# Two of a last group's norms by VectorE, and first products in parts by groups of lines

## The chip, the cores and the metric

One core of a Trainium2 chip runs one program. The metric is the device time of one execution in microseconds (us). The engines named below are PE (TensorE, with PEld for its weight loads), DVE (VectorE), ACT (ScalarE), POOL (GpSimd) and SP (SyncE, which issues most DMAs here). Every engine works through its own instructions in the order in which they were written into its queue and waits on semaphores for the others.

## The reference

Four layers work on an array of 2048 lines of 512 numbers: A, B, A, B. Each one normalizes every line, transforms, and adds the result to the array.

```python
def _A_ref(x, w_r, w_i):
    X = rfft2(x, axes=(-2, -1))
    X = X * (w_r + 1j * w_i)
    return irfft2(X, s=(S, D), axes=(-2, -1))

def _B_ref(u, ...):
    K = einsum("dn,dnl,dn->dl", Cc, exp(logdA[:, :, None] * l), dB).real
    y = irfft2(rfft2(pad(u^T)) * rfft2(pad(K)))[..., :L]     # a long convolution per channel
    return y^T + u * Dskip

x = x + _A_ref(_layernorm(x), A_w_r, A_w_i)
x = x + _B_ref(_layernorm(x), ...)
x = x + _A_ref(_layernorm(x), A_w_r, A_w_i)
x = x + _B_ref(_layernorm(x), ...)
```

The layer norm has no weights: (x - mean) / sqrt(var + 1e-5) over the 512 numbers of a line.

## The kernel before

The array lies on the chip as `x`, 128 partitions by 16 by 512. Here a "line" is one of the 16 indices `s2`, and stands for 128 rows at once. Lines 4i to 4i+3 form group i, four groups in all.

The program has four stages, each with its own list in `ORDER`. The first makes the convolution kernel of layer B (`unit_k`, `rows_k` and others, 32 units) and beside it the first layer A (`forward_a`, `first_a`, `inv_a`), and ends with the norms in front of layer B. The second is the first pass of layer B (r = 0), the third the second layer A, with the norms in front of the last layer, the fourth the second pass of layer B (r = 1).

A stage is a set of pieces, each a generator that emits a few instructions between two `yield`s; what it yields says which engine and buffers it needs next and which events must lie behind it. The class `Clock` writes the order: it keeps a model of the time of each engine, and of all pieces that could go on within a short time from the earliest (the first number of a list in `ORDER`) it takes the one with the lowest rank. A rank is the piece's own number in the first list of its entry, plus a shift from the second list for each later step. The ranks are thus not times; they decide between pieces that are ready together. The order is made when the program is written; on the chip the queues are fixed.

What happens in front of a pass of layer B: `inv_a` adds a line of layer A to `x` (L911 to L913) and takes its statistics on VectorE (`moments`, L591 and L592). When the four lines of a group have theirs, `spread` takes the root on ScalarE (L625), and on VectorE the reciprocal `rs` (L627) and `nb` = -mean * rs (L629). Then `norm_b` writes each line normalized into `xn`, on ScalarE as scale and bias from `rs` and `nb` (L639, in `norm`; L641 is the same norm on VectorE, from the mean and `rs`, which no caller uses before).

`forward_b` multiplies a block of 32 channels of all 16 lines by a table of 128 columns: two matmuls, one for each half of the partitions, each 64 rows by 512 columns (L951). There are 16 such products a pass, and VectorE transposes each result out of PSUM into `P` (L955); the first eight go into the left half. `step_b` works on a half when its eight blocks are there: a product with a table (`spectrum`, L963), in the first pass also one for the convolution kernel's rows (L979 loads them, through a ring of three buffers), the multiplication with the kernel's spectrum (L996, L999, L1003), the product back (L1011), and ScalarE's copy into `P` (L1018). `turn_b` (L1034) and `inv_b` (L1050, L1055) bring the result back to lines; `close_b` takes statistics or writes the output (L1064).

At the end of the first stage a unit ends on GpSimd (L1269, L1270), a product (L1282) and a copy (L1291); `rows_k` multiplies the rows (L1309), transposes them on VectorE (L1313) and stores them (L1316). Then SP loads the tables of layer B (L934, L935).

Of the kernel before, what the change touches and what calls it, by code (L numbers as in the profile page):

```python
# [37 lines left out]
LAND, RATE = 2.0, (320e3, 210e3, 250e3)  # L38

ORDER = [  # L40
    (0.050611, {"load_in": ([-48.73, -49.67, -13.2, 200.39, 38.48], [21.36, 0]),
             "load_n": ([170.88], [17.74, 32.32, 39.11, 0]),
             "load_ra": ([122.74], [-34.24, -26.17, 0]),
             "load_h": ([189.13], [-1.1, 0]),
             "load_da": ([87.12], [11.37, 0]),
             "load_rb": ([156.61], [-6.7, 0]),
             "polar_k": ([188.86], [0, 0, -10.23, 4.9, 30.71, 8.86, -8.44, 0]),
             "octant_k": ([195.76], [0, 0, 30.82, 0]),
             "log_k": ([198.17], [7.12, -1.53, 0]),
             "phase_k": ([54.98], [9.47, -22.65, -34.9, -26.84, -10.4, 0]),  # L50
             "parts": ([-1.02, 52.39, 180.27], [-16.65, -3.98, -14.47, -25.06, -3.65, 0]),
             "load_k": ([0.46, 24.35, 26.66, 90.14, 113.68, 14.97, 134.95, 135.35], [-10.85, -5.26, 0]),
             "exp_k": ([31.12, 30.01, 26.72, -30.41, 4.2, 26.79, 11.64, 78.24, -6.3, 0.57, 130.4, 110.04, 7.61, 12.56, -2.93, 102.4, -2.77, 13.49, 75.18, 23.12, 30.66, 48.47, 2.53, 144.61, -3.85, 206.61, 15.72, 29.43, 103.43, 4.73, 22.38, 4.74, 79.71, 78.57, 136.47, 110.99, 104.63, 0.06, 9.23, -3.76, 152.2, 80.58, 107.2, 21.85, 20.82, 98.84, 202.47, 24.5], [-0.87, -2.09, 0]),
             "unit_k": ([-5.49, 9.8, -46.86, 52.48, -7.95, 46.43, 63.91, 65.15, -59.42, -20.7, 96.11, -25.05, -14.14, 82.98, 95.72, 99.58, 47.51, 48.51, 62.41, 78.63, 79.81, 82.78, 85.31, 89.29, 89.73, 95.21, -3.54, 105.55, 118.51, 120.91, 137.32, 137.55], [34.37, 31.83, 13.78, 42.41, 30.07, 30.15, 32.23, 39.12, 35.89, 0]),
             "rows_k": ([48.24, 146.28, 190.46, 133.31, 5.29, 9.15, 119.72, 143.74], [-28.96, -21.87, -21.87, -15.39, -19.71, -19.24, 0]),
             "sums": ([68.3, 174.15, 8.23, 16.19], [32.48, 30.78, 32.04, 16.99, 13.91, 7.66, 34.05, -0.27, 37.66, 2.46, 0]),
             "spread": ([17.55, 129.21, 18.82, 50.21, 18.68, 37.9, 26.12, 42.83, 81.35], [-14.02, -12.43, 0]),
             "moments": ([48.6, 168.25, 167.06, 170.68], [-35.07, 0]),
             "forward_a": ([237.18, 160.57, 32, 190.87, 212.59, 50.71, -0.81, 157.11, 67.95, -12.81, 211.5, 73.12, 9.09, 134.47, 112.18, 101.62], [-41.16, -32.05, -34.91, -48.86, -16.07, 0]),
             "first_a": ([-4.49, -18.8, 15.57, 3.63, 80.21, 17.42, 26.99, 60.31, 117.89, 120.37, 101.06, 141.83, 161.84, 119.48, 213.35, 138.85], [-2.64, 38.82, -12.59, 0.61, 1.12, 22.42, 1.12, 9.82, -0.59, 0.31, 31.16, 0]),  # L60
             "inv_a": ([119.1, 153.39, 154.78, -12.8, 176.52, 180.93, 165.04, 176.64, 179.21, 212.81, 173.77, 172.16, 165.73, 204.44, 203.24, 205.17], [6.59, 5.52, -33.78, -0.86, 39.16, 4.18, 0]),
             "norm_b": ([134.64, -13.39, 180.42, -19.04, 155.44, 123.24, 118.52, -19.66, -9.73, 62, -15.3, 11.32, -33.63, 181.42, 143.72, 95.73], [3.13, 0]),
             "tables": ([52.58], [-16.4, 0])}),
# [7 lines left out]
    (0.010000, {"load_du": ([164.21], [-44.93, 0]),
             "first_a": ([179.48], [-24.75, -4.44, -14.35, 0, 72.12, 2.11, 1.29, 6.33, 6.76, 0.12, 14.34, 0]),
             "group_a": ([194.01, 232.24, 217.79, 202.63, 238.5, 131.16, 205.2, 199.29, 233.37, 217.41, 208.36, 198.07, 122.44, 202.74, 207.67], [-103.75, -39.32, -54.25, -22.22, -23.2, -100.35, -23.93, -3.71, -36.68, -38.02, -25.08, -23.93, 0]),
             "inv_a": ([180.35, 141.51, 145.93, 197.94, 183.36, 101.66, 176.36, 118.03, 147.61, 232.02, 160.93, 213.63, 186.51, 139.07, 199.6, 146.8], [55.08, 1.48, -4.95, -5.13, 25.36, -6.18, -13.95, 0]),
             "spread": ([177.02, 157.89, 140.63, 190.66], [0, -2.36, 0]),
             "norm_b": ([139.04, 206.02, 221.71, 116.37, 218.26, 121.3, 209.11, 190.78, 125.49, 189.55, 217.69, 200.09, 212.22, 217.5, 116.15, 186.47], [-0.59, 0])}),
    (0.191249, {"forward_b": ([16.74, -30.74, 7.86, -14.65, -23.43, -19.05, -24.28, -7.05, 54.87, 33.03, -16.53, 38.87, 21.87, -22.87, 3.42, -24.9], [-14.33, 68.5, 0]),
             "step_b": ([-48.3, -52.59, -66.06, -59.51, -63.91, -44.14, -38.35, -44.74, -47.06, -34.23, -22.73, -28.22, -1.93, -46.76, 16.96, 16.68], [16.57, 35.26, 26.88, 18.48, 44.4, 11.44, 27.32, 94.94, 0]),
             "turn_b": ([-14.27, -34.14, 44.25, 43.22, 23.59, 43.79, -0.43, 14.42, -40.01, 29.56, 38.77, 2.4], [13.89, 0]),
             "inv_b": ([20.94, 61.81, 32.87, 19.49, -33.55, 25.49, 9.2, -18.63, 60.91, -35.33, 1.86, -32.68, 12.23, 21.87, 69.24, 30.39], [76.77, -10.14, 0]),  # L80
             "close_b": ([-46.35, -28.26, 12.32, -60.23, -24.23, 4.46, -64.62, -57.64], [30.99, 0])}),
# [403 lines left out]
class Net:  # L485
# [451 lines left out]

    def norm_b(self, r, s2, st):

        yield "ACT", self.after((id(st), s2)), self.emitted(("group", 1), 16) if r else self.emitted("product", 32)  # L940
        self.norm(s2, st, True, self.xn[r][:, s2, :])
        self.mark("norm_b", r)

    def forward_b(self, r, i):
# [4 lines left out]
        for h in range(2):
            o = slice(64 * h, 64 * h + 64)  # L950
            nc.tensor.matmul(p[:, 512 * h:512 * h + 512], self.Rb[o, :], self.xn[r][o, :, 32 * i:32 * i + 32], start=True, stop=True)  # L951
# [3 lines left out]
        nc.vector.transpose(self.P[r][e][:, :, o:o + 32].rearrange("p k d -> p d k"), p.rearrange("p (s d) -> p d s", s=32))  # L955
# [557 lines left out]
```

## Time and profile before

| | |
|---|---|
| median of 3 runs | 712.26 us (711.82 to 712.85) |
| profiled execution: its time | 709.7 us |
| profiled execution: its span | 707.9 us |
| mean granted clock of TensorE | 0.927 |
| busy: PE, DVE, ACT, POOL | 580.8, 546.8, 425.8, 314.9 us |
| instructions | 19921 |
| read from and written to HBM | 62.51 and 27.13 MB |
| first product of the first pass of layer B | 344.47 us |
| first product of the second pass of layer B | 598.54 us |

The span goes from the first to the last instruction of the core; the execution's time is 1.8 us longer. A row of the timeline gives start, length, engine, line, operation, output and input by the program's names with their shape, the count, and in brackets how long the engine stood idle before it and for whom. A row of a list of groups gives the busy time of the group, the mean length of one instruction in nanoseconds, and the idle time before it. The granted clock is the share of its full rate that TensorE was given.

### The profile page before, as it was taken

Reading aid. Unit: us, or ns where it says so; the run is one execution under the profiler, and the core shown is the slowest. Engines: PE = TensorE matmul, PEld = TensorE weight load, DVE = VectorE, ACT = ScalarE, POOL = GpSimd, SP = SyncE. Lnnn points to the kernel's source line nnn. Section 1 sums busy time; section 2 is a strip of 40 time slices with the busy share of each in tenths; the row PEclk is TensorE's granted clock in tenths of the full one; section 3 lists DMA queues with packets and bytes.
Section 4 is the critical chain, followed back from the end, with each engine's and each line's share of the span. In section 5 each row is a group of like instructions: output and inputs, shape, how many; then the busy total and the mean of one; then the engine's idle time right before and its main releaser. Section 6 shows DMA issues by size and latency. Waiting matters only on the chain. (4 is left out here: it accounts for less than half of the span.)

```text
span 707.9 us, 19921 instructions
## 1 busy us (share of the span) xinstructions
PE 580.8 (82%) x8424; PEld 372.5 (53%) x8424; DVE 546.8 (77%) x807; ACT 425.8 (60%) x742; POOL 314.9 (44%) x299
## 2 busy tenths in 40 slices
PE   0768988989979999796689998579999981789965
PEld 0767866557544444344236564178778750246621
DVE  1697738787697999988694698876988596984994
ACT  6898369898878969787426553067564436035510
POOL 0652108477294462646024562076665670057710
PEclk9969989999999999887699999779999995999996
DMA  8707443221106520101575876260564013025376
GB/s 211 213 16 239 155 130 96 83 74 53 61 25 193 172 75 2 60 4 62 200 274 186 267 243 191 62 262 1 188 228 146 1 44 134 1 92 170 120 213 189
DMA packets 45857, 90.92 MB, mean 128 GB/s; under 512 B 3944, under 2 KB 25960, under 8 KB 44744
## 3 DMA queue, kind: packets, MB, share of 16 engines
q1 hardware_dynamic: 35016, 77.07, 34.4%
q10 hardware_dynamic: 10752, 12.58, 5.0%
q8 instruction: 66, 1.08, 0.6%
q14 instruction: 23, 0.19, 0.1%
HBM read 62.51 MB, written 27.13 MB: 127 GB/s over the span
## 5 line engine op out<-in xcount | busy, mean ns | idle before, releaser
L1003 POOL TENSOR_TENSOR wk<-wk 128x1024 f32<-128x1024 f32 x32 | 75.9, 2380 | 122.7 <-ACT wk L999 122.7
L1269 POOL TENSOR_TENSOR Y<-wk,Y 128x1024 f32<-128x1024 f32 x32 | 76.7, 2396 | 56.2 <-issue 27.6
L1011 PE MATMUL ps<-wk 32*64 32x256 f32 x2048 | 69.7, 381 | 2.5 <-DVE wk L996 0.9
L951 PE MATMUL ps<-Y,cRb 64*128 64x512 f32 x128 | 37.4, 698 | 29.3 <-ACT Y L639 21.7
L1011 PEld LDWEIGHTS ps<-wk 32*64 32x64 f32 x2048 | 47.1, 131 | 26.0 <-issue 7.7
L996 DVE TENSOR_TENSOR wk<-ps,wk 128x1024 f32<-128x1024 f32 x32 | 38.9, 1220 | 24.9 <-PE ps L963 20.3
L1247 DVE SCALAR_TENSOR_TENSOR wk<-wk,ps 128x1024 f32<-128x1024 f32 x32 | 38.9, 1214 | 22.7 <-ACT wk L1245 22.5
L1282 PE MATMUL ps<-Y 128*32 128x64 f32 x2048 | 39.4, 234 | 14.6 <-POOL Y L1270 11.8
L1231 ACT ACTIVATE Y<-ps 128x1024 f32<-128x1024 f32 x48 | 47.7, 1033 | 4.8 <-PE ps L1215 4.5
L1282 PEld LDWEIGHTS ps<-Y 128*32 128x32 f32 x2048 | 34.2, 119 | 29.9 <-POOL Y L1270 21.1
L1215 PE MATMUL ps<-wk,Y 96*128 96x512 bf16 x128 | 40.6, 394 | 8.4 <-ACT Y L1231 4.8
L1050 PE MATMUL ps<-Y,cRbT 128*64 128x512 f32 x128 | 34.5, 692 | 13.9 <-DMA Y<-yi 7.2
L1270 POOL TENSOR_TENSOR Y<-wk,Y 128x512 f32<-128x512 f32 x32 | 43.6, 1363 | 0.0
L999 ACT COPY wk<-ps 128x512 f32<-128x512 f32 x32 | 18.8, 587 | 41.3 <-PE ps L963 35.0
L1263 DVE TENSOR_TENSOR Y<-ps,Y 128x1024 f32<-128x1024 f32 x32 | 38.8, 1213 | 3.2 <-PE ps L1282 2.1
L827 POOL TENSOR_TENSOR x<-x 128x257 f32<-128x257 f32 x16 | 11.6, 723 | 64.4 <-PE ps L850 35.6
L1034 DVE STREAM_TRANSPOSE Y<-Y 128x1024 f32<-128x1024 f32 x16 | 36.7, 2315 | 4.3 <-ACT Y L1018 4.3
L951 PEld LDWEIGHTS ps<-Y,cRb 64*128 64x128 f32 x128 | 12.3, 213 | 52.6 <-ACT Y L639 24.1
L1245 ACT ACTIVATE wk<-ps,magic 128x1024 f32<-128x1024 f32 x32 | 35.5, 1120 | 6.2 <-PE ps L1215 5.9
L1252 ACT ACTIVATE ps<-wk 128x1024 f32<-128x1024 f32 x32 | 32.8, 1026 | 6.3 <-DVE wk L1247 2.4
L1255 ACT ACTIVATE wk<-wk,quarter 128x1024 f32<-128x1024 f32 x32 | 36.4, 1137 | 0.1
L907 PE MATMUL ps<-wk,cRaT 128*128 128x512 f32 x64 | 34.3, 629 | 2.1 <-ACT wk L882 1.9
(232 smaller groups left out, 1631.2 us busy)
## 6 DMA issues: line engine op xcount, KB each, us to landing
yk<-wk SPq DMA_DIRECT2D x8, 1024.0 KB
wk<-yk SPq DMA_DIRECT2D x16, 512.0 KB
khat<-wk ACTq DMA_DIRECT2D x16, 512.0 KB
wk<-khat SPq DMA_DIRECT2D x16, 512.0 KB
Y<-in_W_dram SPq DMA_DIRECT2D x12, 515.0 KB
x<-in_cPa_dram SPq DMA_DIRECT2D x16, 384.0 KB
Y<-in_cGa_dram SPq DMA_DIRECT2D x12, 384.0 KB
x<-in_W_dram SPq DMA_DIRECT2D x16, 258.0 KB
```

The costliest lines, as they stand in the source:

```text
L951: nc.tensor.matmul(p[:, 512 * h:512 * h + 512], self.Rb[o, :], self.xn[r][o, :, 32 * i:32 * i + 32], start=True, stop=True)
L996: nc.vector.tensor_tensor(t0, X[:, 0, :, None, :].to_broadcast(four), kh[:, 0, None, :, :].to_broadcast(four), op=OP.mult)
L1003: nc.gpsimd.tensor_tensor(t1, xi[:, :, None, :].to_broadcast(four), kh[:, 1, None, :, :].to_broadcast(four), op=OP.mult)
L1011: nc.tensor.matmul(v[i // 2][64 * a:64 * a + 64, 512 * (i % 2):512 * (i % 2) + 256], self.Ib[o, g, a, b, :], t[o, x, k, :], start=n == 0, ...
L1034: self.nc.vector.transpose(y.rearrange("p s d -> p d s"), self.P[r][e][:, :, o:o + 32].rearrange("p k d -> p d k"))
L1215: self.nc.tensor.matmul(p, f[:, c:c + 128], self.oh[:k, o:o + 512], start=True, stop=True)
L1231: nc.scalar.activation(m[:, :, 1024:] if i == 2 else m[:, i, :1024], p.rearrange("p (i m) -> p i m", i=2) if i == 2 else p, AF.Exp)
L1247: nc.vector.scalar_tensor_tensor(s, c, MAGIC, p, op0=OP.subtract, op1=OP.subtract)
L1263: nc.vector.tensor_tensor(E[:, 1, :1024], p, m[:, :1024], op=OP.mult)
L1269: nc.gpsimd.tensor_tensor(E[:, 0, :1024], c, m[:, :1024], op=OP.mult)
L1270: nc.gpsimd.tensor_tensor(rows(E[:, 0, 1024:]), back(c[:, 512:]), rows(m[:, 1024:]), op=OP.mult)
L1282: nc.tensor.matmul(pk[32 * j:32 * j + 32, 64 * e:64 * e + 64], E1[:, r, i, :], E2[:, r, i], start=r == 0, stop=r == 1)
```

## The change

`norm_b` puts lines 8 and 9 on VectorE (L641) and the other fourteen on ScalarE as before, and marks its event by group. `forward_b` waits for the four groups one by one. For two of the sixteen products of a pass (4 and 6 in the first, 1 and 15 in the second: those with the lowest ranks) it emits the columns of lines 0 to 7 and 12 to 15 first, behind groups 0, 1 and 3, and the columns of lines 8 to 11 in a step of their own behind group 2. The others wait for all four groups and go in one part. All ranks of all four lists are new, and so are the short times (0.010000 becomes 0.016166 in the third list, the others change by under 2%).

```diff
@@ ORDER: all four lists, here the forward products and some of the others @@
-    (0.106371, {"forward_b": ([29.41, 45.28, 85.57, 67.58, 7.03, 50.48, 14.98, 21.28, 109.8, 98.41, 90.83, 85.95, 131.45, 144.47, 19.4, 145.79], [-5.6, -0.98, 0]),
+    (0.105136, {"forward_b": ([7.3, 35.97, 8.14, 55.24, -7.1, 73.99, -3.89, 11.45, 102.42, 103.84, 84.86, 41.36, 78.66, 130.53, 89.7, 155.34], [0, 0, 0, 0]),
...
+             "inv_a": ([158.52, 158.55, 184.82, 25.76, 196.79, 223.38, 200.56, 217.82, 215.08, 255.07, 213.57, 196.11, 216.97, 239.72, 239.02, 246.73], [-20.37, -20.71, -60.82, -27.92, -0.75, -20.44, 0]),
...
+             "inv_a": ([167.42, 193.28, 178.13, 195.04, 195.65, 166.7, 158.76, 170.71, 230.07, 233.32, 166.74, 194.05, 192.84, 151.98, 177.23, 184.96], [22.67, -40.15, 11.7, -15.49, 2.92, -5.29, 19.8, 0]),
...
-    (0.191249, {"forward_b": ([16.74, -30.74, 7.86, -14.65, -23.43, -19.05, -24.28, -7.05, 54.87, 33.03, -16.53, 38.87, 21.87, -22.87, 3.42, -24.9], [-14.33, 68.5, 0]),
+    (0.192792, {"forward_b": ([-39.37, -60.29, -23.5, -16.3, -32.87, -30.14, -15.98, -5.61, -36.95, 70.23, 21.35, -28.69, 54.59, 34.15, -31.13, -41.02], [-0.34, 2.72, 0, 0]),
...
+FIRST = (4, 6), (1, 15)
...
     def norm_b(self, r, s2, st):
 
-        yield "ACT", self.after((id(st), s2)), self.emitted(("group", 1), 16) if r else self.emitted("product", 32)
-        self.norm(s2, st, True, self.xn[r][:, s2, :])
-        self.mark("norm_b", r)
+        act = s2 not in (8, 9)
+        yield "ACT" if act else "DVE", self.after((id(st), s2)), self.emitted(("group", 1), 16) if r else self.emitted("product", 32)
+        self.norm(s2, st, act, self.xn[r][:, s2, :])
+        self.mark("norm_b", r, s2 // 4)
 
     def forward_b(self, r, i):
 
         nc = self.nc
-        yield "PE p:u", self.after(("norm_b", r), 16)
-        p = self.psum("u")
-        for h in range(2):
-            o = slice(64 * h, 64 * h + 64)
-            nc.tensor.matmul(p[:, 512 * h:512 * h + 512], self.Rb[o, :], self.xn[r][o, :, 32 * i:32 * i + 32], start=True, stop=True)
+        normed = [self.after(("norm_b", r, k), 4) for k in range(4)]
+        parts = ((0, 8), (12, 16)), ((8, 12),)
+        if i not in FIRST[r]:
+            parts = ((0, 16),),
+        for k, part in enumerate(parts):
+            if k == 0:
+                yield "PE p:u", normed[0], normed[1], normed[3], *normed[2:3] * (len(parts) == 1)
+                p = self.psum("u")
+            else:
+                yield "PE", normed[2]
+            for h in range(2):
+                o = slice(64 * h, 64 * h + 64)
+                for a, b in part:
+                    nc.tensor.matmul(p[:, 512 * h + 32 * a:512 * h + 32 * b], self.Rb[o, :], self.xn[r][o, a:b, 32 * i:32 * i + 32], start=True, stop=True)
```

More of the change, by code (lines that the diff above doesn't have):

```diff
@@ L40 @@
 ORDER = [
[L41 to L63, printed above, removed]
@@ L71 @@
[L71 to L76, printed above, removed]
@@ L77 @@
[L77 to L81 removed]
+    (0.050611, {"load_in": ([2.14, -31.49, 60.38, 195.95, 62.39], [-5.34, 0]),
+             "load_n": ([162.77], [21.6, 34.91, 21.6, 0]),
+             "load_ra": ([111.95], [-8.08, -14.65, 0]),
+             "load_h": ([138.52], [-14.4, 0]),
+             "load_da": ([122.57], [-9.59, 0]),
+             "load_rb": ([118.83], [-21.66, 0]),
+             "polar_k": ([180.49], [0, -15.92, -10.39, 4.9, 6.15, 0.23, -15.07, 0]),
+             "octant_k": ([-12.75], [18.15, 17.08, 71.2, 0]),
+             "log_k": ([125.26], [13.96, -7.38, 0]),
+             "phase_k": ([82.15], [-18.39, -50.67, -60.78, -68.43, -44.46, 0]),
+             "parts": ([96.23, 121.16, 171.19], [29.55, 16.72, 5.01, -3.36, -47.62, 0]),
+             "load_k": ([5.09, 26.52, 38.33, 89.4, 129.67, 134.53, 17.57, 178.23], [4.96, 1.73, 0]),
+             "exp_k": ([30.04, 4.85, 39.82, 0.5, 7.05, 21.91, 8.12, 114.54, 9.72, -11.15, 158.96, -1.55, 22.25, 18.32, -65.23, 8.09, -12.99, 16.82, 18.92, 20.05, -19.18, 49.28, -12.85, 150.98, 3.52, 17.05, 115.34, -8.23, -2.37, 199.57, 32.51, 1.41, 34.85, 76.23, 129.16, 113.74, 97.49, 112.01, -1.27, 8.21, -12.83, 140.78, 133.71, -13.21, 125.47, 105.46, -1.42, -33.61], [-1.6, -0.73, 0]),
+             "unit_k": ([-7.31, 10.27, -40.19, 49.73, -12.86, -6.94, 66.86, 70.18, -99.11, -8.78, 103.47, -30.03, -33.82, 76.29, 84.35, 110.62, 41.65, 57.36, 64.29, 81.46, 79.97, 85.01, 87.58, 87.74, 88.39, 91.69, 61.12, 94.43, 102.28, 114.56, 128.37, 134.44], [37.07, 32.4, 26.45, 46.25, 33.05, 33.13, 35.21, 42.1, 38.01, 0]),
+             "rows_k": ([38.49, 144.37, 196.76, 142.7, -45.1, 2.59, 38.57, -12.82], [-30.33, -13.55, -27.23, -15.5, -23.48, -11.99, 0]),
+             "sums": ([116.72, 84.23, 27.49, 23.58], [5.29, 23.25, 2.88, -1.55, 4.82, 5.29, 11.65, 5.29, 27.57, -19.83, 0]),
+             "spread": ([4.69, 75.48, -22.97, 94.08, 11.95, 71.94, -24.27, 113.82, -3.16], [11, 8.59, 0]),
+             "moments": ([162.83, 151.37, 116.25, 133.96], [-22.25, 0]),
+             "forward_a": ([193.6, 186.31, 16.84, 148.27, 107.84, 111.78, -0.37, 9.05, 83.39, -5.4, 107.22, 116.39, -17.2, 125.87, 145.17, 70.04], [-12.92, 0, -2.69, 0.82, 15.59, 0]),
+             "first_a": ([-15.91, -11.05, 8.37, -2.97, 87.71, 10.51, 22.14, 56.52, 105.03, 131.34, 99.53, 134.5, 157.68, 122.1, 202.53, 125.71], [26.37, 43.51, -2.16, 10.99, 11.14, 44.66, 17.33, 22.39, 9.43, 10.42, 34.93, 0]),
+             "inv_a": ([158.52, 158.55, 184.82, 25.76, 196.79, 223.38, 200.56, 217.82, 215.08, 255.07, 213.57, 196.11, 216.97, 239.72, 239.02, 246.73], [-20.37, -20.71, -60.82, -27.92, -0.75, -20.44, 0]),
+             "norm_b": ([-23.5, -12.28, 191.19, 71.08, -21.33, 152.29, 126.27, 107.8, -18.26, -14.58, -25.67, 169.56, -6.26, 160.12, -32.74, -12.32], [16.65, 0]),
+             "tables": ([185.33], [-3.26, 0])}),
```

21 lines of the change are left out of this document (15 added, 6 removed).

## The prediction

> **What bounds the kernel now.** I read the page's busy shares, then the engines by stretches, then the timeline at the two places that the change touches, then the chain that ended last. The stretches first (columns: busy time and count of PE, PEld, DVE, ACT, POOL, then the granted clock, DMA share, GB/s):
>
> ```profile
> PE 580.8 (82%) x8424; PEld 372.5 (53%) x8424; DVE 546.8 (77%) x807; ACT 425.8 (60%) x742; POOL 314.9 (44%) x299
> ...
> 280.00:320.00 40.00, 35.53 (x504) 16.85 (x508) 37.36 (x50) 32.26 (x38) 20.28 (x12) 0.88 0.08 28
> ...
> 557.00:594.00 37.00, 24.68 (x128) 16.34 (x126) 34.79 (x86) 17.02 (x40) 23.05 (x57) 0.86 0.23 85
> 594.00:598.50 4.50, 0.00 (x0) 0.00 (x0) 0.36 (x3) 4.05 (x7) 0.00 (x0) 0.50 0.00 0
> 598.50:624.00 25.50, 19.59 (x109) 6.90 (x116) 23.31 (x14) 0.59 (x1) 0.37 (x1) 0.89 0.00 1
> 624.00:655.00 31.00, 29.90 (x881) 17.74 (x873) 18.18 (x14) 14.26 (x26) 22.83 (x10) 1.00 0.48 152
> ```
>
> No engine is full on average, but the stages have different owners. VectorE is busy 34.8 of 37 us while the second layer A closes, and 23.3 of 25.5 us while layer B's first products are turned; TensorE is the full one in the steps behind that (29.9 of 31). Between them lie 4.5 us in which TensorE does nothing, VectorE 0.36 us, and only ScalarE works. The timeline there, in front of the second pass:
>
> ```profile
> 589.19 5.74 ACT L639 ACTIVATE Y<-x,nb,rs 128x512 f32<-128x512 f32 x8
> ...
> 593.84 0.18 DVE L592 BATCH_NORM_AGGREGATE mv<-st 128x2 f32<-128x6 f32 x1
> 594.84 0.28 ACT L625 ACTIVATE rs<-mv,eps 128x4 f32<-128x4 f32 x1
> 595.15 0.18 DVE L627 RECIPROCAL rs<-rs 128x4 f32<-128x4 f32 x1 [1.13 <-ACT rs L625]
> 595.37 0.16 DVE L629 SCALAR_TENSOR_TENSOR nb<-mv,rs 128x4 f32<-128x4 f32 x1
> 595.57 2.93 ACT L639 ACTIVATE Y<-x,nb,rs 128x512 f32<-128x512 f32 x4 [0.44 <-DVE nb L629]
> 598.54 3.78 PE L951 MATMUL ps<-Y,cRb 64*128 64x512 f32 x8 [16.79 <-ACT Y L639]
> 600.69 1.94 DVE L955 STREAM_TRANSPOSE Y<-ps 128x1024 f32<-128x1024 f32 x1 [5.16 <-PE ps L951]
> ```
>
> Twelve of the sixteen lines are normalized at 594.93 (589.19 + 5.74). The last group of four has its statistics at 594.02, its root only when ScalarE is through with eight norms, and then four norms in a row, 2.93 us. The first product waits for all sixteen; VectorE stands 5.16 us until it ends. In front of the first pass the same picture, with TensorE and VectorE also at the last kernel rows (L1309, L1313):
>
> ```profile
> 335.43 4.10 PE L1309 MATMUL ps<-wk,cRk 32*128 32x512 f32 x16 [1.29 <-ACT wk L1291]
> ...
> 339.19 1.50 ACT L639 ACTIVATE Y<-x,nb,rs 128x512 f32<-128x512 f32 x2
> 339.26 1.91 DVE L1313 STREAM_TRANSPOSE wk<-ps 128x1024 f32<-128x1024 f32 x1 [1.05 <-PE ps L1309]
> ...
> 341.04 0.14 DVE L627 RECIPROCAL rs<-rs 128x4 f32<-128x4 f32 x1
> 341.23 0.16 DVE L629 SCALAR_TENSOR_TENSOR nb<-mv,rs 128x4 f32<-128x4 f32 x1
> 341.31 1.91 DVE L1313 STREAM_TRANSPOSE wk<-ps 128x1024 f32<-128x1024 f32 x1
> 341.49 2.93 ACT L639 ACTIVATE Y<-x,nb,rs 128x512 f32<-128x512 f32 x4 [0.79 <-DVE nb L629]
> ...
> 344.47 3.75 PE L951 MATMUL ps<-Y,cRb 64*128 64x512 f32 x8 [4.93 <-ACT Y L639]
> ...
> 346.67 3.67 DVE L955 STREAM_TRANSPOSE Y<-ps 128x1024 f32<-128x1024 f32 x2 [3.45 <-PE ps L951]
> ```
>
> The chain that ended last (start, length, what) runs through the norms, the product and VectorE's transposes, up to the first step:
>
> ```profile
> 621.69 1.81 DVE Ya L955
> 623.54 1.00 PE ps L963 x25
> ```
>
> So whatever makes the first transpose earlier moves everything behind it, as long as nothing else becomes late.
>
> **The change, part by part.** Durations are of the profiled execution: span 707.9, own time 709.7, 2.6 below the median of 712.26 that I forecast against. I take differences only.
>
> First, two norms of lines 8 and 9 go to VectorE. Group 2 stays the last group: the inverse products of lines 8 and 9 carry the highest ranks of the new third list (230.07, 233.32; next is 195.65), and line 9 that of the first (255.07; next is 246.73). ScalarE then has two of four norms: 2.93/4 = 0.73 each, so 1.47 us less. What VectorE pays for a norm, a two-operand TENSOR_SCALAR over 128x512 f32 with the scalars in memory, is not in the trace; the same operation with fixed scalars is:
>
> ```profile
> L1091 DVE TENSOR_SCALAR Y<-Y 128x512 f32<-128x512 f32 x3 | 1.3, 426 | 0.1
> L911 DVE TENSOR_TENSOR x<-x,ps 128x512 f32<-128x512 f32 x32 | 21.6, 674 | 6.4 <-PE ps L907 6.4
> ```
>
> 0.43 from below, 0.67 from above (a full pass with two streams); I take 0.5, nearest to L1091, so 1.0 for two. They need the reciprocal, not nb. In front of the second pass VectorE has nothing else: 595.53 to 596.5 (at worst 596.9), before ScalarE's second norm ends at 597.04. They cost nothing there.
>
> Second, the first two products are split: lines 0 to 7 and 12 to 15 first, then 8 to 11. The weights are loaded again for each part. How a product runs at this place shows in its weight loads:
>
> ```profile
> 599.56 0.34 PEld L951 LDWEIGHTS ps<-Y,cRb 64*128 64x128 f32 x2 [0.51 <-issue]
> 600.41 0.34 PEld L951 LDWEIGHTS ps<-Y,cRb 64*128 64x128 f32 x2 [0.51 <-issue]
> ...
> 600.60:604.02 3.42, 3.42 (x12) 1.36 (x10) 3.33 (x2) 0.00 (x0) 0.00 (x0) 0.50 0.00 0
> ```
>
> A pair each 0.85 us at a granted clock of 0.50, two pairs a product: 1.70. From its start to the transpose are 600.69 - 598.54 = 2.15, so 0.45 us lie behind the last column. The first part has 384 of 512 columns: 1.28 by columns, 1.54 where the short stretch is bound by its weight pair (0.34 twice for 0.43 of columns); I take 1.4. The second part is 0.43 by columns, 0.68 by weights; I take 0.55.
>
> Second pass: TensorE is empty, so the first parts start at 594.95. I expect both first parts before either second part, since the second first part is ready while group 2 still waits: 594.95 + 2.8 = 597.75, later than the norms (597.04). Second part and tail: 598.75 (598.39 to 599.16) against 600.69, that is 1.9 us less (1.5 to 2.3). Were the first product finished before the second one starts, it would be 597.04 + 0.55 + 0.45 = 598.05, 2.6 less. Behind that, transposes are 1.74 apart and a product 1.70 even at the low clock, so TensorE keeps pace. The new ranks put the eighth left-half product twelfth, as the chain has it now (products 1, 15, 0, 8, 4, ... up to 7), so the first step moves by the same amount.
>
> First pass: twelve lines are ready at 340.69, TensorE is through with L1309 at 339.53. First parts to 343.5. ScalarE's two norms end at 342.96. VectorE's two stand either ahead of the second L1313 (341.4 to 342.4) or behind it (343.22 to 344.2). The transpose starts at 343.5 + 1.0 = 344.5 or at 345.2, against 346.67: 2.2 or 1.5 less; I take 1.9 (1.3 to 2.5). Behind it, SP issues kernel rows and tables in order, and an L1313 pushed back by 1 us pushes these loads by as much. Is the load late then?
>
> ```profile
> 356.00:358.00 2.00, 1.41 (x8) 0.30 (x4) 2.00 (x2) 0.00 (x0) 0.00 (x0) 1.00 0.98 401
> 358.00:360.00 2.00, 1.38 (x34) 0.50 (x32) 2.00 (x2) 0.00 (x0) 0.00 (x0) 1.00 0.10 39
> ...
> wk<-yk SPq DMA_DIRECT2D x4, 512.0 KB
> ...
> 359.05 1.10 PE L963 MATMUL ps<-wk 64*32 64x256 f32 x32 [0.62 <-DVE Y L955]
> ```
>
> The burst ends near 358. Three of these loads of 512 KB fit in the ring of three before a product frees one, so the first is in about 1.05 MB earlier, 2.6 us at 401 GB/s: 355.4. The first product with kernel rows (359.05, which waits for VectorE) has 3.6 us of room; it moves to 357.1, and even with a load 1 us later the room holds. If that cover went, the pass would keep only the second pass's 1.9.
>
> Third, all ranks are new. Their effect outside the two places can't be read from the profile of before; I put it at 0, and take for its size the grain of the first stage, one pair of GpSimd products:
>
> ```profile
> 328.55 2.37 POOL L1269 TENSOR_TENSOR Y<-wk,Y 128x1024 f32<-128x1024 f32 x1
> ...
> 330.88 1.27 POOL L1270 TENSOR_TENSOR Y<-wk,Y 128x512 f32<-128x512 f32 x1
> ...
> 332.20 1.94 PE L1282 MATMUL ps<-Y 128*32 128x64 f32 x64 [2.46 <-POOL Y L1270]
> ```
>
> 2.37 + 1.27 = 3.6 us for the unit that ends the stage; TensorE waits 2.46 us for it.
>
> Sum: -1.9 - 1.9 = -3.8; 712.26 - 3.8 = 708.5. With the bounds of both terms, 707.5 to 709.5.
>
> **Rivals.** (a) More than forecast: the new order puts the last group's root ahead of some norms (0.82 us, 594.02 to 594.84), and L1313 not ahead of the reciprocal (341.04 instead of about 339.3, of which ScalarE's earlier norms leave about 1.2), and the second part of the first product ahead of the other first part (0.7). Together up to 2.7 more: 705.8. For it: these waits are in the trace. Against: the change doesn't name them.
>
> (b) No change: the new order lets one unit of the first stage end a pair later (3.6): 712.1. For it: from 280 to 320 TensorE and VectorE are busy 35.5 and 37.4 of 40 us, so the list has little slack. Against: nothing in the change lengthens the units.
>
> (c) Slower: the same mechanism with two units, whose products (L1282) and rows then follow behind the point where VectorE and ScalarE are done: 2 x 3.6 - 3.8 = +3.4, 715.7. It decides from 5.2 us of delay on (3.8 + 1.4).
>
> (d) The norms on VectorE meet GpSimd. A TENSOR_SCALAR beside a GpSimd product is stretched here:
>
> ```profile
> 320.68 1.27 POOL L1270 TENSOR_TENSOR Y<-wk,Y 128x512 f32<-128x512 f32 x1
> 320.85 1.66 DVE L1248 TENSOR_SCALAR wk<-wk 128x1024 uint32<-128x1024 uint32 x1
> ...
> L1248 DVE TENSOR_SCALAR wk<-wk x32: 693/695/2730, 96.0 to 324.2; 128x1024 uint32<-128x1024 uint32 x32
> ```
>
> 0.69 alone, 1.66 here, 2.73 at most: up to 2.0 more per norm. The Trainium skill, "SBUF — State Buffer", section "Who interferes with whom", has the rule: such an operation in its two-port mode and GpSimd exclude each other, and the later one is blocked for the whole instruction. By that rule the trace agrees at 320.85, and the rule speaks against giving norms to VectorE. Against the rival: in the first place GpSimd ends its last pair at 332.15, nine us ahead of the norms, and in the second it is busy 0.00 of the 4.5 us. If the new order left a GpSimd pair at the first place, the norms would end 2.0 later and that pass's gain would be gone: 710.4.
>
> (e) The change doesn't do what it says, since line 9's group isn't last or the parts are emitted together: only the two shorter norm rows remain, 2 x 1.47 = 2.9, 709.3, within the forecast.
>
> **How the numbers follow.** The forecast with (e) 0.46, (a) 0.14, (d) 0.04, all faster: 0.64. (b) 0.15. (c) 0.21. A difference under 0.2% (1.4 us) is about what a measurement of this kernel can't tell from none. The range reaches into (a) with 704.0 and towards (c) with 714.5, and leaves out about 0.1 at each end. The forecast's own range is 707.5 to 709.5.
>
> **What would show it.** Right: in front of each pass two L639 instead of four for the last group and two TENSOR_SCALAR from L641 of about 0.5 us; L951 starting within 0.1 us of the twelfth norm, in short pieces, at clock 0.50; in the second pass about 4.7 us from the last statistics to the first L955, where it is 6.67 now (594.02 to 600.69). Wrong: those waits shorten, but the first L955 of the first pass stands later than 346.67, since the first stage ends later; or the steps behind the transposes wait for loads; or the tail after the last step grows.

## The result, and the profile after

The changed kernel takes 727.9 us (median of five executions, 725.71 to 730.59) beside 711.15 for the kernel before on the same chip: a ratio of 1.0243, interval 1.0203 to 1.0284. Slower by 17 us, where 3.8 us less was predicted. One more execution of the changed kernel (954.52 us at a mean clock of 0.558) and one of e9 below (749.95 us at 0.777) were slow, and no median or ratio here counts them. In the two profiled executions the mean granted clock is the same (0.928 and 0.927), and the work nearly so; the head of the page of the changed kernel:

```profile
span 728.7 us, 19977 instructions
...
PE 584.8 (80%) x8456; PEld 377.2 (52%) x8456; DVE 548.3 (75%) x811; ACT 423.2 (58%) x738; POOL 314.4 (43%) x299
```

TensorE is 4.0 us busier, with 32 more matmuls, VectorE 1.5 us (four norms), ScalarE 2.6 us less. Most of the 20.8 us that the span grew by is therefore waiting. The span can be cut at six events that both traces have: the end of the last statistics in front of a pass (L592 before, L593 after), the first transpose out of PSUM (L955, L966), and the end of the pass's last `spectrum` product (L963, L974). All in us; the last five columns are experiments that are told below:

| stretch | before | after | e5 | e7 | e8 | e9 | e11 |
|---|---|---|---|---|---|---|---|
| start to last statistics, first pass | 338.21 | 349.90 | 338.74 | 337.90 | 340.17 | 336.74 | 339.52 |
| to its first transpose | 8.45 | 11.26 | 11.22 | 9.82 | 8.13 | 7.19 | 6.88 |
| to its last `spectrum` product | 88.46 | 95.05 | 94.37 | 89.09 | 87.59 | 89.07 | 88.73 |
| to last statistics, second pass | 158.89 | 161.89 | 161.00 | 161.78 | 157.36 | 159.54 | 159.74 |
| to its first transpose | 6.67 | 4.72 | 4.72 | 4.72 | 5.24 | 5.37 | 4.52 |
| to its last `spectrum` product | 71.73 | 72.05 | 72.28 | 71.76 | 71.68 | 71.89 | 71.87 |
| to the end of the span | 35.48 | 33.83 | 34.97 | 35.53 | 34.33 | 35.80 | 34.64 |
| span | 707.9 | 728.7 | 717.3 | 710.6 | 704.5 | 705.6 | 705.9 |

Four rows hold the loss: +11.7 in the first stage, +2.8 at the head of the first pass, +6.6 in that pass behind the head, +3.0 up to the second pass. The head of the second pass brought 1.95, as predicted. What makes the stretch up to the second pass longer stays open; it goes with the new third list, since all kernels that have this list take 161.0 to 161.9 us there, and those with the old one 157.4 to 159.9.

**First stage, +11.7.** Until 230 us the two traces run within 2.3 us of each other. Then, in the changed kernel (columns as in the prediction's first fence):

```profile
235.00:240.00 5.00, 0.98 (x20) 0.33 (x12) 5.00 (x6) 3.29 (x4) 5.00 (x3) 0.80 0.60 170
240.00:245.00 5.00, 0.00 (x0) 0.00 (x0) 1.03 (x3) 0.00 (x0) 1.82 (x2) 0.50 0.68 211
```

and in the kernel before:

```profile
235.00:240.00 5.00, 4.17 (x75) 1.82 (x74) 4.93 (x9) 4.99 (x7) 4.58 (x3) 1.00 0.64 184
240.00:245.00 5.00, 5.00 (x104) 2.57 (x105) 4.69 (x8) 4.98 (x7) 0.23 (x1) 1.00 0.72 245
```

TensorE stands still. What it waits for is in its timeline and in the queue of SP, both of the changed kernel:

```profile
212.88 27.83 SPq L560 DMA_DIRECT2D x<-in_A_x_dram  x32
240.81 0.79 SPq L1217 DMA_DIRECT2D Y<-spe  x1
245.12 1.04 PE L1226 MATMUL ps<-wk,Y 96*128 96x512 bf16 x2 [9.14 <-DMA Y<-spe]
```

L1226 multiplies a batch of factors, one of eight, that `load_k` (L1217) brings in through a ring of two buffers. The load stands in SP's queue behind 32 reloads of `x`, and TensorE waits 9.14 us for it. In the kernel before, SP's queue has the same picture at the same place:

```profile
211.42 27.12 SPq L559 DMA_DIRECT2D x<-in_A_x_dram  x32
...
233.64 0.79 PE L1215 MATMUL ps<-wk,Y 96*128 96x512 bf16 x2
...
238.65 0.79 SPq L1206 DMA_DIRECT2D Y<-spe  x1
```

yet the first product of the same batch, at 233.64, waits for nothing. The difference is which batch is the late one. The rows don't name the batches; the ranks of `load_k` for batches 0 to 7 tell them apart:

```diff
-             "load_k": ([0.46, 24.35, 26.66, 90.14, 113.68, 14.97, 134.95, 135.35], [-10.85, -5.26, 0]),
+             "load_k": ([5.09, 26.52, 38.33, 89.4, 129.67, 134.53, 17.57, 178.23], [4.96, 1.73, 0]),
```

Beside batch 0, the lowest rank was batch 5's (14.97) and is now batch 6's (17.57). That batch is loaded at the very start (90.94 us) and keeps one of the two buffers until its turn. So the load behind the reloads was batch 6's, wanted at about 260 us; it is now batch 5's, wanted at 236.

**Head of the first pass, +2.8.** The timeline of the changed kernel; the rows of before stand in the prediction:

```profile
347.08 1.28 ACT L626 ACT_TABLE_LOAD   x1
...
349.28 0.35 ACT L1302 COPY wk<-ps 128x256 f32<-128x256 f32 x1
349.68 4.10 PE L1320 MATMUL ps<-wk,cRk 32*128 32x512 f32 x16 [3.78 <-ACT wk L1302]
349.72 0.18 DVE L593 BATCH_NORM_AGGREGATE mv<-st 128x2 f32<-128x6 f32 x1
...
353.51 1.91 DVE L1324 STREAM_TRANSPOSE wk<-ps 128x1024 f32<-128x1024 f32 x1 [1.17 <-PE ps L1320]
355.28 0.47 DVE L642 TENSOR_SCALAR Y<-x,mv,rs 128x512 f32<-128x512 f32 x1
355.67 1.88 DVE L1324 STREAM_TRANSPOSE wk<-ps 128x1024 f32<-128x1024 f32 x1
357.41 0.47 DVE L642 TENSOR_SCALAR Y<-x,mv,rs 128x512 f32<-128x512 f32 x1
357.70 6.63 PE L962 MATMUL ps<-Y,cRb 64*128 64x256 f32 x36 [3.91 <-DVE wk L1324]
361.16 3.70 DVE L966 STREAM_TRANSPOSE Y<-ps 128x1024 f32<-128x1024 f32 x2 [3.28 <-PE ps L962]
```

The last copy of the first stage (L1302) stands behind the table load, root and a norm on ScalarE, and TensorE waits 3.78 us for it. The two VectorE norms are 0.47 us each, but one stands between the two kernel-row transposes and one behind both. The first parts do not start with the twelfth norm: by the program's semaphores they wait for the second L1324, which reads the PSUM pair that they write (PSUM is the memory that TensorE's products are written into; a pair is the two times 512 columns of one product). So they begin at 357.70, when both norms are nearly done, and from there to the first transpose are 3.46 us (two first parts and a second one), where a whole product took 2.20 (344.47 to 346.67).

**First pass behind the head, +6.6.** VectorE's and TensorE's rows, first of the kernel before, then of the changed one:

```profile
366.57 5.71 DVE L955 STREAM_TRANSPOSE Ya<-ps 128x1024 f32<-128x1024 f32 x3
...
368.62 1.99 PE L1011 MATMUL ps<-wk 32*64 32x256 f32 x64 [0.21 <-DVE Ya L955]
```

```profile
381.08 10.69 DVE L966 STREAM_TRANSPOSE Ya<-ps 128x1024 f32<-128x1024 f32 x6
...
386.60 0.66 PE L1022 MATMUL ps<-wk 32*64 32x256 f32 x8 [0.58 <-DVE Ya L966]
388.32 3.57 PE L1022 MATMUL ps<-wk 32*64 32x256 f32 x56 [1.06 <-DVE Ya L966]
```

After the first two steps' products the planner put six transposes of right-half products in a row instead of three. These products hold PSUM pairs that the product back (L1022) needs; it goes out piecemeal as transposes free them. During the gap the granted clock falls:

```profile
385.00:390.00 5.00, 3.35 (x46) 1.56 (x52) 5.00 (x4) 0.00 (x0) 0.00 (x0) 0.82 0.22 90
390.00:395.00 5.00, 5.00 (x144) 3.05 (x136) 2.83 (x3) 2.71 (x4) 0.00 (x0) 0.84 0.20 52
```

and the 56 matmuls take 3.57 us, where 64 took 1.99 before.

**Head of the second pass, -1.95.** The changed kernel:

```profile
616.30 2.91 ACT L640 ACTIVATE Y<-x,nb,rs 128x512 f32<-128x512 f32 x4
...
617.91 0.18 DVE L593 BATCH_NORM_AGGREGATE mv<-st 128x2 f32<-128x6 f32 x1
619.11 0.28 ACT L626 ACTIVATE rs<-mv,eps 128x4 f32<-128x4 f32 x1
619.26 6.87 PE L962 MATMUL ps<-Y,cRb 64*128 64x256 f32 x36 [14.32 <-ACT Y L640]
...
619.72 1.00 DVE L642 TENSOR_SCALAR Y<-x,mv,rs 128x512 f32<-128x512 f32 x2
619.84 1.52 ACT L640 ACTIVATE Y<-x,nb,rs 128x512 f32<-128x512 f32 x2 [0.44 <-DVE nb L630]
622.82 1.91 DVE L966 STREAM_TRANSPOSE Y<-ps 128x1024 f32<-128x1024 f32 x1 [2.10 <-PE ps L962]
```

TensorE starts 0.05 us after the twelfth norm (619.21), VectorE's two norms end 0.64 us ahead of ScalarE's, and the first transpose stands 4.73 us behind the last statistics (618.09).

### The profile page after: what moved, and what is told of

The parts are those of the page before. It is cut to its first block, busy times and chain, and to the rows that moved or that the text cites. A ratio compares the mean times of both kernels' runs of the same rounds, so it can differ in the third digit from the quotient of the medians.

```text
span 728.7 us, 19977 instructions
## 1 busy us (share of the span) xinstructions
PE 584.8 (80%) x8456; PEld 377.2 (52%) x8456; DVE 548.3 (75%) x811; ACT 423.2 (58%) x738; POOL 314.4 (43%) x299
## 2 busy tenths in 40 slices
DMA packets 45858, 90.94 MB, mean 125 GB/s; under 512 B 3944, under 2 KB 25960, under 8 KB 44744
## 5 line engine op out<-in xcount | busy, mean ns | idle before, releaser
L1022 PE MATMUL ps<-wk 32*64 32x256 f32 x2048 | 72.2, 388 | 4.1 <-DVE Ya L966 2.4
L1022 PEld LDWEIGHTS ps<-wk 32*64 32x64 f32 x2048 | 47.9, 133 | 28.7 <-issue 6.3
L962 PE MATMUL ps<-Y,cRb 64*128 64x512 f32 (+2 forms) x160 | 37.7, 593 | 28.0 <-ACT Y L640 14.3
L1226 PE MATMUL ps<-wk,Y 96*128 96x512 bf16 x128 | 42.2, 416 | 17.9 <-DMA Y<-spe 11.5
L1293 PE MATMUL ps<-Y 128*32 128x64 f32 x2048 | 40.5, 238 | 14.7 <-POOL Y L1281 12.0
L1293 PEld LDWEIGHTS ps<-Y 128*32 128x32 f32 x2048 | 35.1, 122 | 30.3 <-POOL Y L1281 20.4
L1061 PE MATMUL ps<-Y,cRbT 128*64 128x512 f32 x128 | 32.8, 663 | 17.2 <-DMA Y<-yi 16.6
L962 PEld LDWEIGHTS ps<-Y,cRb 64*128 64x128 f32 x160 | 16.1, 227 | 48.7 <-DVE Y L966 18.2
L828 POOL TENSOR_TENSOR x<-x 128x257 f32<-128x257 f32 x16 | 11.6, 728 | 64.2 <-PE ps L851 35.9
L1320 PE MATMUL ps<-wk,cRk 32*128 32x512 f32 x128 | 32.5, 674 | 5.3 <-ACT wk L1302 4.3
```

The source lines that it names most:

```text
L962: nc.tensor.matmul(p[:, 512 * h + 32 * a:512 * h + 32 * b], self.Rb[o, :], self.xn[r][o, a:b, 32 * i:32 * i + 32], start=True, stop=True)
L1022: nc.tensor.matmul(v[i // 2][64 * a:64 * a + 64, 512 * (i % 2):512 * (i % 2) + 256], self.Ib[o, g, a, b, :], t[o, x, k, :], start=n == 0, ...
L1061: nc.tensor.matmul(q[64 * h:64 * h + 64, :], self.RbT[:, t:t + 64], self.turned[r][e][:, o:o + 512], start=True, stop=True)
L1226: self.nc.tensor.matmul(p, f[:, c:c + 128], self.oh[:k, o:o + 512], start=True, stop=True)
L1293: nc.tensor.matmul(pk[32 * j:32 * j + 32, 64 * e:64 * e + 64], E1[:, r, i, :], E2[:, r, i], start=r == 0, stop=r == 1)
```

## The experiments

The theory: the order in which the instructions stand, not the norms and not the parts, makes the kernel slower, above all the late factor load. The rival: the norms on VectorE or the four parts cost what was gained. Ratios are to the kernel before, run on the same chip.

| run | ratio | interval |
|---|---|---|
| e1 both, lists of before | 0.9983 | 0.9968 to 0.9998 |
| e2 new lists alone | 1.0250 | 1.0236 to 1.0264 |
| e3 two load ranks exchanged | 1.0269 | 1.0253 to 1.0285 |
| e4 norms alone, lists of before | 1.0052 | 1.0037 to 1.0068 |
| e5 two loads exchanged, order kept | 1.0140 | 1.0091 to 1.0189 |
| e6 last copy first, order kept | 1.0263 | 1.0231 to 1.0295 |
| e7 e5 and e6, first pass in another order | 1.0034 | 1.0009 to 1.0059 |
| e8 as e4, first pass in the order of before | 0.9957 | 0.9932 to 0.9982 |
| e9 parts alone, order of before | 0.9972 | 0.9948 to 0.9996 |
| e10 as e8, again | 0.9969 | 0.9947 to 0.9991 |
| e11 as e1, again | 0.9967 | 0.9945 to 0.9990 |
| e12 as e11, norms ahead of a transpose | 0.9994 | 0.9966 to 1.0022 |

### e1 and e2: the lists apart from the code

e1 keeps the changed functions and takes all four lists from before (for the split products with their first shift doubled, since they have one step more). e2 keeps the new lists and takes the functions back:

```diff
@@ e1: the lists, here one line of the four @@
-    (0.105136, {"forward_b": ([7.3, 35.97, 8.14, 55.24, -7.1, 73.99, -3.89, 11.45, 102.42, 103.84, 84.86, 41.36, 78.66, 130.53, 89.7, 155.34], [0, 0, 0, 0]),
+    (0.106371, {"forward_b": ([29.41, 45.28, 85.57, 67.58, 7.03, 50.48, 14.98, 21.28, 109.8, 98.41, 90.83, 85.95, 131.45, 144.47, 19.4, 145.79], [-5.6, -0.98, 0]),
...
+                shifts = shifts[:1] + shifts
@@ e2: the code @@
-FIRST = (4, 6), (1, 15)
+FIRST = (), ()
...
-        act = s2 not in (8, 9)
+        act = True
```

> The whole change (two norms on VectorE, first products in parts) with the four rank lists of before; every queue then equals that of before but for the moved norms and the split products. Theory L (the new lists lost the time, the change itself gains): the first stage ends as before, the pass 1 boundary shrinks by 1.9 us as it did with the new lists, the pass 0 boundary gives 0 to 1.5: 707.5 to 710 where before has about 711, ratio 0.995 to 0.999. Theory C (the change itself costs, by first parts that wait for PSUM and by norms behind the kernel rows' transposes): 715 or more.

> The new rank lists alone: all norms on ScalarE and no product in parts. Theory L: slower than before by most of the 18 us, 722 to 732, with the wait of TensorE for the factor load near 235 to 245 us in its trace. Theory C: 709 to 714, as before.

e1 runs at 0.9983, e2 at 1.0250. The lists alone cost as much as the whole change, and the code alone, in the order of before, costs nothing. That excludes the rival as the cause of the 17 us. The trace of e2 has the same wait for the factor load,

```profile
244.51 1.04 PE L1226 MATMUL ps<-wk,Y 96*128 96x512 bf16 x2 [9.10 <-DMA Y<-spe]
```

and its first stage ends at 349.76. Behind the head of the first pass it loses 3.0 us (91.47) and not 6.6: four transposes stand in its row and not six. So the row of six belongs to lists and code together, and that e2 comes out at the same total is in part chance.

### e3: exchange the ranks of two loads

```diff
-             "load_k": ([5.09, 26.52, 38.33, 89.4, 129.67, 134.53, 17.57, 178.23], ...
+             "load_k": ([5.09, 26.52, 38.33, 89.4, 129.67, 17.57, 134.53, 178.23], ...
```

> The changed kernel with one edit: the ranks of the factor loads of batches 5 and 6 exchanged, so that batch 5 is the one that is loaded early and held in the second buffer, as before. Theory L1 (the load of batch 5 stands behind 32 reloads of x in SP's queue and TensorE waits 9 to 11 us for it): 729 - 10 = 717 to 721, and the wait near 235 to 245 us is gone. Rival (the factor load is late only since the first stage is late by other things): 727 to 731.

1.0269: a miss. The wait is gone, as the stretches of this run show,

```profile
235.00:240.00 5.00, 5.00 (x102) 2.49 (x94) 4.86 (x7) 4.08 (x5) 1.75 (x3) 1.00 0.66 190
240.00:245.00 5.00, 5.00 (x93) 2.48 (x96) 4.90 (x11) 4.99 (x7) 3.34 (x2) 1.00 0.82 261
```

but the planner, whose model of time had changed, wrote the rest of the stage in another order. The product of its last unit (L1293) ends at 346.82, and the copy of it now stood behind 6.4 us of ScalarE's other work:

```profile
344.88 1.93 PE L1293 MATMUL ps<-Y 128*32 128x64 f32 x64 [1.62 <-POOL Y L1281]
353.20 0.35 ACT L1302 COPY wk<-ps 128x256 f32<-128x256 f32 x1
353.60 4.11 PE L1320 MATMUL ps<-wk,cRk 32*128 32x512 f32 x16 [6.79 <-ACT wk L1302]
```

A change of a rank is thus no experiment on one wait here. From e5 on the order was held (e4 still has its order from the ranks): the sequence in which a kernel's pieces go out was written down and replayed, with only the named entries changed.

```diff
-            t, p = min((e for e in ready if e[0] <= self.now + near), key=lambda e: e[1][:2])
+            at = int(script.pop(0))
+            t, p = next(e for e in ready if e[1][1] == at)
```

### e4: the norms alone

The lists of before, two norms of the last group on VectorE, no parts. Against e1:

```diff
-FIRST = (4, 6), (1, 15)
+FIRST = (), ()
```

> Lists of before, norms of lines 8 and 9 on VectorE, no product in parts. In this kernel VectorE's queue has the six right-half transposes of the first pass in one row behind the second step's product, as in the changed kernel, where before has three, three products and then the others. Theory R (that row costs pass 0 about 6 us, since the product back waits for PSUM that the right-half products hold): 711 - 1.5 (pass 1) - 0.5 + 6 = 715 to 717. Rival (that row is harmless and pass 0 lost its time by late loads): 708 to 710.

1.0052, above e1, although e1 has the same norms and the parts besides; its 713.2 us are somewhat below the 715 to 717 expected. The trace shows the same row of six transposes in the first pass as in the changed kernel:

```profile
367.27 10.76 DVE L968 STREAM_TRANSPOSE Ya<-ps 128x1024 f32<-128x1024 f32 x6
...
372.76 0.66 PE L1024 MATMUL ps<-wk 32*64 32x256 f32 x8 [0.58 <-DVE Ya L968]
374.49 1.96 PE L1024 MATMUL ps<-wk 32*64 32x256 f32 x56 [1.06 <-DVE Ya L968]
```

So the row of six isn't a matter of the new lists as such; the planner falls into it from the old ones too, when the norms' events come at other times.

### e5, e6 and e7: mend the changed kernel one place at a time

All three replay the order of the changed kernel. e5 exchanges the loads of batches 5 and 6. e6 puts the last copy (L1302) ahead of the table load and root (L626). e7 does both and takes the order of e1 for the first pass of layer B. Of the sequence of pieces:

```diff
@@ e5 and e7, first stage @@
-load_k(0), load_k(6)
+load_k(0), load_k(5)
...
-load_k(5)
+load_k(6)
@@ e6 and e7, first stage, ScalarE at the end @@
-spread (L626), norm_b (L640), last copy (L1302)
+last copy (L1302), spread (L626), norm_b (L640)
@@ e7, first pass of layer B @@
-the sequence of the changed kernel
+the sequence of e1
```

> The changed kernel with every engine's queue exactly as it is, but batch 5 of the factors (not 6) in the early load and batch 6 in the load behind the 32 reloads of x. Theory L1 (which batch is loaded early decides whether TensorE waits 9 to 10 us near 235 to 245 us): ratio to before 1.009 to 1.012 where the changed kernel has 1.024. Rival (the swapped load only moves the stall, to batch 6 or to the reloads): 1.02 or more.

> The changed kernel with one move on ScalarE's queue: the copy of the last unit's product (L1302) ahead of the table load, root and norm at the end of the first stage, as before. Theory A (the copy waits 2.3 us there and the kernel rows' product, which the first pass waits for, with it): 2 to 2.5 us less than the changed kernel, ratio 1.020 to 1.022. Rival (the last group's norms, 1.3 us later by it, set the start of the pass): 1.023 to 1.025.

> The changed kernel with three mends: batch 5 loaded early, the copy first, and the first pass of layer B in the order that the lists of before give it (three right-half transposes behind the second step's product instead of six). Theory L (these three places hold the loss): 729 - 10 - 2.3 - 5 = 711 to 713, ratio 0.998 to 1.004. Rival (the loss is spread over the whole new order): 1.008 or more.

e5: 1.0140, above the 1.009 to 1.012 expected, which its interval reaches into. The product that waited 9.14 us now has its factors at 234.79 (the load behind the reloads is still there, but it is batch 6's):

```profile
234.79 0.71 PE L1240 MATMUL ps<-wk,Y 96*128 96x512 bf16 x2
...
239.54 0.79 SPq L1231 DMA_DIRECT2D Y<-spe  x1
```

The first stage ends at 338.74 instead of 349.90, and every later stretch is within 0.9 us, but for the tail (+1.1). By the ratios the load costs 1.0243 - 1.0140 = 1.0%, 7.3 us; by the two traces 11.2 in its stage, of which 1.2 lie ahead of the wait (batch 4's products begin at 208.57 instead of 209.78). Single executions of one kernel differ by some us (725.71 to 730.59 for the changed one, 716.98 to 723.72 for e5), so the size lies between these, and the sign and place are sure.

e6: 1.0263, a miss: no gain to be seen. In its trace the copy comes 2.74 us earlier (346.54), and the first transpose 1.6 us (359.56 instead of 361.16), since a reciprocal of the last group now holds VectorE's queue ahead of the first kernel-row transpose, and its root stands behind four norms:

```profile
346.94 3.91 PE L1334 MATMUL ps<-wk,cRk 32*128 32x512 f32 x16 [1.46 <-ACT wk L1316]
...
348.41 2.91 ACT L654 ACTIVATE Y<-x,nb,rs 128x512 f32<-128x512 f32 x4
...
351.54 0.18 DVE L642 RECIPROCAL rs<-rs 128x4 f32<-128x4 f32 x1 [1.81 <-ACT rs L640]
...
351.83 1.93 DVE L1338 STREAM_TRANSPOSE wk<-ps 128x1024 f32<-128x1024 f32 x1
```

Why even these 1.6 us do not appear in the times is open; they are within the spread of single runs. This trace is also 2.7 us shorter behind the head of the first pass (92.38), where nothing was changed; the last section comes back to that.

e7: 1.0034. By the table the first pass behind its head is back at 89.09, its head at 9.82. From e5 to e7 the ratio falls by 1.06%, 7.5 us; the rows of the table that the two edits touch fall by 5.28 + 1.40 = 6.7. Of the copy nothing was seen in e6's time, so most of this is the row of six transposes, with the low clock that came with it in e5 (last section). What is left against e11 (0.0067 or 4.8 us) is in two rows of the table: 2.94 at the head of the first pass, where the parts still stand behind the kernel-row transposes, and 2.04 in the stretch with the second layer A, whose new list e7 keeps.

### e8: the norms alone, without the row of six

```diff
@@ against e4, first pass of layer B @@
-the sequence of e4
+the sequence of before
```

> Norms of lines 8 and 9 on VectorE, no parts, with the first pass in the order of before: against the earlier kernel with these norms (1.0052) only the order of eight rows on VectorE and nine on TensorE is changed. Theory R (the row of six right-half transposes costs about 4 us): ratio 0.997 to 1.000. Rival (the norms on VectorE themselves cost it): 1.004 to 1.006.

0.9957 against 1.0052 for e4: the order of the first pass alone is worth 0.95%, 6.7 us (by its repetition e10 0.83%, 5.9; by the traces 5.4 and 4.1 us behind the head, from 92.98 to 87.59 and 88.86). VectorE has three in a row again and the product back goes out whole:

```profile
368.19 5.70 DVE L982 STREAM_TRANSPOSE Ya<-ps 128x1024 f32<-128x1024 f32 x3
370.24 1.99 PE L1038 MATMUL ps<-wk 32*64 32x256 f32 x64 [0.21 <-DVE Ya L982]
```

### e9 to e12: what the two halves bring when the order stays

All on one chip. e9 has the parts alone, e10 repeats e8, e11 repeats e1. e12 takes e11 and exchanges, in VectorE's queue, the two norms of the first pass with the second kernel-row transpose.

```diff
@@ e9, against e11 @@
-        act = s2 not in (8, 9)
+        act = True
@@ e12, against e11: VectorE's queue in front of the first pass @@
-L1340 STREAM_TRANSPOSE, L658 TENSOR_SCALAR, L658 TENSOR_SCALAR
+L658 TENSOR_SCALAR, L658 TENSOR_SCALAR, L1340 STREAM_TRANSPOSE
```

> All four norms on ScalarE as before, the first two forward products of each pass in parts, every queue otherwise in the order of before. Theory A (the parts help at both boundaries: a part runs while TensorE would wait, so the first transpose comes 0.5 to 0.7 us sooner in pass 1 and about 1.5 us sooner in pass 0): 708 us where before is 710, ratio 0.997 to 0.999. Theory B (four parts per product cost more TensorE time and semaphores than one whole product, and what comes sooner at the head is waited for behind it): 1.000 to 1.004. The step in the trace: last statistics to first transpose in pass 1, 6.67 us in before, 6.0 to 6.2 here by both; what differs is the last spectrum of pass 0 and the end.

> The norms by VectorE alone, in the order of before, again, beside the parts alone and both on one chip. Theory A (each half gains by itself and they add): 0.9957 again, and both together lower still, 0.994. Theory B (the norms alone are all the gain): 0.9957 again and both together no lower.

> The whole change with the four lists of ranks of before, again, on the same chip. Theory A (halves add): 0.994 to 0.996. Theory B (the parts take back what the norms give): 0.998, as in its first run.

> The whole change in the order of before, with the two VectorE norms of pass 0 put ahead of the second kernel-row transpose in VectorE's queue (two rows of one queue change places, nothing else). Theory A (VectorE's order at the head of pass 0 counts): the two norms end 1.9 us sooner; the first whole product no longer waits for them and the first transpose comes 0.5 to 1 us sooner, 0.1 to 0.2% below e11. Theory B (the first parts wait for the second kernel-row transpose anyway, because it reads the PSUM banks that they write, and that transpose now ends 0.9 us later): the first transpose comes 0.5 to 0.9 us later than in e11, the time equal to e11 or 0.1% above.

0.9972, 0.9969 and 0.9967: each half brings about 0.3%, and both together 0.3%. The interval of e11 reaches to both forecasts, 0.994 to 0.996 and 0.998, so it decides between neither. At the heads the halves nearly add, as the table's second and fifth rows show: e8 (the norms) -0.32 and -1.43, e9 (the parts, expected at about -1.5 and -0.5 to -0.7) -1.26 and -1.30, e11 (both) -1.57 and -2.15. These are -1.8, -2.6 and -3.7 us, the last of which is what was predicted. In the time of e11 are 2.3 us (710.46 times 0.0033; 0.7 to 3.9 by the interval), in e1's 1.2 (0.1 to 2.3). The stretches that nobody touched are longer in these traces by 1.3 (first stage) and 0.85 (second layer A) us, but the same stretch differs as much between e8 and e10, which are one kernel (last statistics at 340.17 and 338.60). So whether the rest of the gain is lost somewhere or only hidden by this spread is open.

e12 is 0.9994. The first part of its expectation came: the norms end 1.77 us sooner, and the first transpose stands 6.01 us behind the last statistics, 0.87 less than in e11. The reason behind theory B did not hold: the first parts run from 340.71 on, ahead of the second kernel-row transpose. But the time did not follow, and from the first transpose to the last `spectrum` product are 90.30 us, 1.57 more than in e11. The first product with kernel rows comes only 0.16 us sooner, since it now waits for its load:

```profile
343.49 1.92 DVE L1340 STREAM_TRANSPOSE wk<-ps 128x1024 f32<-128x1024 f32 x1
345.44 0.36 SPq L1343 DMA_DIRECT2D yk<-wk  x1
...
358.61 1.10 PE L990 MATMUL ps<-wk 64*32 64x256 f32 x32 [1.41 <-DVE Y L982]
```

In e11 it starts 12.37 us after the first transpose, here 13.14, with 1.41 us idle instead of 0.61. VectorE's transposes came sooner and not later, so what ended the wait is not the one named but the load of the kernel rows, whose store went out 0.84 us later than in e11 (344.60). SP's queue itself waits for that load before it issues the fourth load of kernel rows, and this wait ends at 358.53, 0.08 us ahead of the product; in e11 it ends at 358.26, 0.51 ahead, and in the kernel before at 356.86, 2.2 ahead. From the issue of the store to this product are 13.17 us.

## Why the prediction was wrong

**The step that failed** is the third term: "Third, all ranks are new. Their effect outside the two places can't be read from the profile of before; I put it at 0, and take for its size the grain of the first stage, one pair of GpSimd products". Measured, with e2: the ranks alone cost 2.5%, 17.7 us. The term was put at 0 with a grain of 3.6; it is five times that grain. And part of it could be read: that SP is full from 211.42 to 238.54 with 32 reloads stands in the trace of before, that a factor load comes right behind it (238.65) too, and which batch that is stands in a list of the change. For the first stage the prediction asked which GpSimd unit could come late, and not which DMA stood behind which in SP's queue. In e2's trace the first stage is 11.6 us longer; the rest is behind the head of the first pass (3.0) and, with its cause open, in the second layer A (2.3).

**Rival (c)** had the right sign and stage, but not the mechanism: not units of GpSimd that end a pair later, but one load that lets the whole chain wait. Its price of 715.7 was bounded by a grain from the wrong engine.

**The second pass's term** was right in its mechanism: 4.73 us from the last statistics to the first transpose (4.7 predicted), two norms 1.00 (1.0), first parts 0.05 behind the twelfth norm (within 0.1), VectorE's norms ahead of ScalarE's. That the sum is right to 0.1 us is luck: TensorE starts 1.17 us behind the statistics, where 0.93 was reckoned (594.95 - 594.02), and the first transpose follows after 3.56 and not 3.80 (598.75 - 594.95). Behind that nothing came late: to the last product with the kernel table are 72.05 us, 71.73 before.

**The first pass's term** failed in the changed kernel: 2.8 more instead of 1.9 less. Two steps of it were wrong there. "First parts to 343.5" took TensorE and twelve norms for all that a part waits for; it also needs the PSUM pair, and in this order the kernel-row transposes had it. And the norms' place, ahead of the second L1313 or behind it, was priced as 0.7 us between the two cases, while the copy ahead of them, pushed behind the root, cost more. In the order of before the term holds, by the second of its two cases: in e11 the parts start at 340.78, the VectorE norms stand behind the second kernel-row transpose, and the first transpose comes 6.88 us behind the last statistics, 1.57 less than before (1.3 to 2.5 predicted; that case has 345.2 - 338.21 = 6.99).

**Rival (d)** did not come: the four norms took 0.47 to 0.54 us each, with no GpSimd product beside them.

**The cover of the kernel rows' load** was put at 3.6 us. By SP's own wait the first load was in at 356.86 in the kernel before and not at 355.4, which leaves 2.2 (359.05 - 356.86). It is 0.5 in e11 and used up in e12, where the norms went ahead; in the changed kernel it held, with the product at 373.56 and the load in at 370.72.

**Rival (e)**, only the shorter norm rows, is close to what e10 measured: 0.31%, 2.2 us, for 2.9 predicted.

No version beats e8 to e11 by more than the intervals; norms alone or parts alone, in the order of before, give the same 0.3%.

## What to carry to other kernels

When a change comes with a new order, price the order first: go through each queue, the DMA queues above all, and ask for every load behind a long burst which data it brings and when these are wanted. A planner's ranks change more than their own step, so an experiment on one wait must hold the rest of the order, by replaying it with one entry moved (e3 against e5). And an engine that starts earlier needs its output buffer as well as its inputs: look up what last read it.
